# First pair's lam products on VectorE, and four W1 blocks of the next pair in places of product 7's operand

## The chip, the cores and the metric

The kernel runs on 1 core of a Trainium2 chip. The metric is the device time of one execution in microseconds (us). The engines are TensorE (PE; PEld is its weight load), VectorE (DVE), ScalarE (ACT), GpSimd (POOL) and SyncE (SP); each works through its own queue in order.

## The reference

Grouped-query attention (batch 8, 16 query heads, 4 key heads, 384 tokens, head size 64), whose output is x, followed by an MLP block:

```
x   = softmax(q k^T / 8) v                 # as (8, 384, 1024)
a1  = alpha1 * x + beta1
tok = w_tok @ a1                           # over the 384 tokens
u   = x + lam * tok
a2  = alpha2 * u + beta2
ch  = relu(a2 @ w_ch1) @ w_ch2             # 1024 -> 4096 -> 1024
out = u + lam * ch
```

Inputs and output are float32; the kernel multiplies in bf16.

## The kernel before

**Pairs.** The eight batches are taken as four pairs. Each pair goes through two big products: the first one (a2 with W1) and the second one (hidden with W2). Both are made of seven smaller products, numbered 1 to 7, by a Strassen-like scheme: operands are summed or subtracted first, the results afterwards. The attention and the token step of the next pair (function `side`) are woven into the second product of the current one, piece by piece, so that TensorE always has something to do.

**The order is written by hand.** `put(ps, phase, at, function, ...)` files a call under pair `ps`, phase 0 (first product) or 1 (second product) and step `at`. `steps(ps)` runs the pair's generator, and after each step runs what is filed under its number. In the first pair's second product (`second_product`, matmuls C L752) there are 21 turns of four steps: a turn is one product number and one third of the tokens (`turns`), with 16 matmuls of 128x512. Turns 9 to 20 are products 3, 6, 7 and 4, so product 4 has steps 72 to 83. Batch 3 (`C` side of the next pair) is filed 38 steps later than its table says: its step 22 is step 60 of the phase.

**The side's work.** Per piece p of 128 columns: scores (L260) and exponentials (ACT L269), attention output (L295), on DVE the reciprocal L300, x L303 and a1 L309, then the token matmuls `tok` (L324, L328), and on DVE L331 (u) and L334 (a2, in `obuf`). For some pieces of batch 3, `turn` transposes a2 on TensorE (L398) and ACT copies it out (L400). Scores, attention output, tokens and turns take turns on three PSUM banks (`three`), named sc in the trace. DVE also makes the sums of W2 blocks (`sum_w2`, L499), of the hidden (L603) and, near the end of the phase, of W1 blocks (`sum_w1`, L510 and L515) and of the turned a2 (`sums_a`, L448 to L450).

**Results.** ACT copies product sums to hT (L764) or back into a PSUM bank (L744), and DVE adds (L767). Finished parts are appended to `later`. `flush` takes them from there: `scaled` multiplies a 128x512 part by lam in place (L790) and `store` adds it to the output in memory with an accumulating DMA on POOL's queue (L442). In the first pair (`lead`) the product L790 is POOL's, in later pairs DVE's. Of the first pair's twelve parts, nine are flushed in its second product: the first three, of product 2, as soon as they can be, then those of products 6 and 7 from turn 17 on. The three of product 4 are flushed in the next pair's first product, one in each of its groups 1, 2 and 3.

**W1 blocks.** The next pair's first product (L831) needs 16 W1 blocks of 128 x 8 x 256 in the order `order1` = 0, 8, 1, 9, 2, 10, 3, 11, 4, 12, ..., two for each of its eight groups of 9.1 us. `load_w1` (L183) casts a block from memory into one of six slots of the ring `w1`, by a DMA on POOL's queue. Loads wait in `queue`, and `pump` issues the next one when a slot is freed. The W2 blocks of the second product use the same ring and three slots of `pad`.

**Product 7's operand.** The sums for the first pair's product 7 lie in `home(0)` to `home(3)`, four places of 128x2048 at the end of `arena`. The last read of them is in turn 17. The next pair's hidden is written over them in its groups 6 and 7.

Of the kernel before, what the change touches and what calls it, by code (L numbers as in the profile page):

```python
# [13 lines left out]
def kernel(  # L14
# [21 lines left out]
    nc = tc.nc  # L36
# [4 lines left out]
    MUL = mybir.AluOpType.mult  # L41
# [8 lines left out]
    P = 128  # L50
# [125 lines left out]

    w1src = moe_w_ch1.rearrange("(dt di) nf -> di dt nf", di=P)
    w2src = moe_w_ch2.rearrange("(nt ni) d -> ni nt d", ni=P)
    w1_slots, w1_free = {}, list(range(RING))

    def load_w1(c):
        w1_slots[c] = w1_free.pop(0)
        nc.gpsimd.dma_start(out=w1[:, w1_slots[c]], in_=w1src[:, :, c * CW * P:(c + 1) * CW * P])  # L183

    def bank(shape, tag, name, dtype=f32):
        if tag == "mm":
# [27 lines left out]
    def side(b):  # L214
# [192 lines left out]
        def put(k, *m):  # L407
            at.setdefault(k, []).append(m)
# [3 lines left out]
        for p in range(NP):  # L412
            put((4, 10, 14, 18, 24, 29, 33, 35)[p], av, p)
            put((8, 15, 17, 22, 27, 32, 36, 38 if b % 2 else 39)[p], tok_flip, p)
            if by_pe(p):
                put(((13, 20, 22, 28, 34, 37, 40, 42) if b == 3 else (0, 0, 0, 0, 0, 36, 39, 41))[p], turn, p)
        return at

    def loads(b):
# [84 lines left out]
        free(raw["12", c][0])  # L504

    def sum_w1(g, o):
        a, c = w1[:, w1_slots[g]], w1[:, w1_slots[g + NCH // 2]]
        H1, H2 = slice(0, NDT // 2), slice(NDT // 2, NDT)
        if o == 7:
            tt(out=c[:, H1], in0=c[:, H2], in1=c[:, H1], op=SUB)  # L510
            tb[g, 7], tb[g, 1], tb[g, 2], tb[g, 3] = c[:, H1], a[:, H1], a[:, H2], c[:, H2]
            return
        tb[g, o] = t = piece().rearrange("p (a c) -> p a c", a=NDT // 2)
        x, y = {5: (c[:, H1], a[:, H1]), 6: (c[:, H2], tb.get((g, 5))), 4: (a[:, H2], tb.get((g, 6)))}[o]
        tt(out=t, in0=x, in1=y, op=SUB)  # L515
# [58 lines left out]
    for name, cs, slots in (("12", (0, 1), w1_free), ("12", (2, 3), pad_free), ("22", (0,), pad_free), ("22", (1, 2, 3), w1_free),  # L574
                            ("again", (0,), w1_free), ("again", (1,), pad_free), ("again", (2, 3), w1_free)):
        queue += [(load_w2, name, c, slots) for c in cs]
    queue += [(load_w1, c) for c in order1[:4]]
    for i in range(1, NB):
        heads = [(load_w1, c) for c in order1[:4]] if i + 1 < NB else []
        queue += [(load_w1, c) for c in order1[4:]] + [(fetch, i, n) for n in range(SLOTS - 2)] + heads[:2]  # L580
        queue += [(fetch, i, n) for n in (SLOTS - 2, SLOTS - 1)] + heads[2:]

    IDENT = mybir.ActivationFunctionType.Identity
# [144 lines left out]
    def second_product(acc, later, flush, scaled):  # L728
        pad_free[:] = [RING + 1, RING, RING + 2]
        pump()  # L730
        s2, s1, s5, s3 = ([snaps[:, (NST * i + ms) * 512:(NST * i + ms + 1) * 512] for ms in range(NST)] for i in range(4))
        names = {1: "11", 2: "21", 3: "22", 5: "12", 6: "12", 7: "11", 4: "again"}
        xs_ = {}
        turns = ((1, 0), (1, 1), (2, 0), (2, 1), (1, 2), (5, 0), (2, 2), (5, 1), (5, 2),
                 *((o, ms) for o in (3, 6, 7, 4) for ms in range(NST)))

        def begin(o, ms):
            if o == 2:
                xs_[o, ms] = xs_[1, ms]
                return  # L740
            xs_[o, ms] = x = acc.tile([P, 512], f32, tag="acc", name="C", bufs=2)
            under = {3: s5, 6: s1, 7: s1, 4: s1}.get(o)
            if under:
                nc.scalar.copy(out=x, in_=under[ms])  # L744

        for k, (o, ms) in enumerate(turns):
            if (o, ms) not in xs_:
                begin(o, ms)
            x = xs_[o, ms]
            for t in range(NH):  # L750
                slot, rhs = raw[names[o], t // 4]
                nc.tensor.matmul(out=x, lhsT=lead_hid[:, t, FIRST2[o], ms * P:(ms + 1) * P],  # L752
                                 rhs=rhs[:, t % 4 * 512:(t % 4 + 1) * 512], start=(o in (1, 5) and t == 0), stop=(t == NH - 1),
                                 skip_group_check=True)
                if t % 4 == 3 and ms == NST - 1 and (o in (2, 3) or o == 4 and slot < RING):
                    free(slot)
                if t % 4 == 3 and t < NH - 1:
                    if t == 7 and turns[k + 1:] and turns[k + 1][0] in (3, 6, 7, 4):
                        begin(*turns[k + 1])
                    if t % 8 == 3 and later and (later[0][1] == 1 or k > 16 and later[0][1] != 4):  # L760
                        flush(1)
                    yield 1
            to = {1: s1, 2: s2, 5: s5, 3: s3, 6: s1, 7: s1, 4: s3}[o][ms]
            nc.scalar.copy(out=to, in_=x)  # L764
            if o in (6, 7):
                to, base = (s2[ms], s3[ms]) if o == 6 else (s5[ms], s5[ms])
                tt(out=to, in0=x, in1=base, op=ADD)  # L767
            if o in (2, 6, 7, 4):
                later.append((scaled, 1 if o == 2 else o, int(o in (7, 4)), ms, int(o in (6, 7)), to))
            yield 1  # L770

    def pair(i):
# [14 lines left out]

        def scaled(o, b, ms, dw, t):
            if o != 2 or not last:
                (nc.gpsimd if lead else nc.vector).tensor_tensor(out=t, in0=t, in1=lam_t[:, dw * 512:(dw + 1) * 512], op=MUL)  # L790
            store(b, ms, dw, t)

        def flush(n=9):
# [24 lines left out]
        for g in range(NH // 2):  # L818
            X, Y, snap = {}, {}, {}
            for k, (o, e) in enumerate(SEQ1):  # L820
                t = 2 * g + e
                lo, hi = bias1[:, t:t + 1], bias1[:, NH + t:NH + t + 1]
                if o == 1:
                    X[e] = pairs["X"].tile([P, 512], f32, tag="X", name="X", bufs=2)
                if o == 7:
                    Y[e] = pairs["Y"].tile([P, 512], f32, tag="Y", name="Y", bufs=2)
                if o == 2:
                    Z = pairs["Z"].tile([P, 512], f32, tag="Z", name="Z", bufs=4)
                ps = (X[e] if o in (1, 6, 5, 3) else Y[e] if o in (7, 4) else Z)[:, :S]
                for dt in range(NDT // 2):  # L830
                    nc.tensor.matmul(out=ps, lhsT=tb[g, o][:, dt, e * P:(e + 1) * P], rhs=opb(LEFT1[o])[:, dt],  # L831
                                     start=(o in (1, 2, 7) and dt == 0), stop=(dt == NDT // 2 - 1), skip_group_check=True)
                if o in (1, 6, 5):
                    q = ((2 if g % 2 else 8) + 2 * (1, 6, 5).index(o) + e) % 12 * S
                    snap[o, e] = snaps[:, q:q + S]
                    nc.scalar.activation(out=snap[o, e], in_=ps, func=IDENT, bias=hi if o == 5 else lo)  # L836
                if o == 5:
                    tt(out=hid[:, t, 1], in0=Y[e][:, :S], in1=snap[5, e], op=ADD)  # L838
                elif o == 2:
                    tt(out=hid[:, t, 0], in0=ps, in1=snap[1, e], op=ADD)  # L840
                elif o == 3:
                    nc.scalar.activation(out=hid[:, t, 4], in_=ps, func=RELU, bias=hi)  # L842
                elif o == 4:
                    tt(out=hid[:, t, 2], in0=ps, in1=snap[6, e], op=ADD)
                if k == 7 and 0 < g < 4:
                    flush(1)
                if (o, e) in ((2, 1), (3, 1)):
                    free(w1_slots.pop(g if o == 2 else g + NCH // 2))
                if k == 3 and g == 0:
                    tt(out=opb(6), in0=opb(4), in1=opb(5), op=SUB)  # L850
                if k == 2 and g == 0:
                    sum_w1(0, 4)
                if k in (2, 5, 8, 11) and g + 1 < NH // 2:
                    sum_w1(g + 1, {2: 5, 5: 7, 8: 6, 11: 4}[k])
                ts = slice(2 * g, 2 * g + 2)
                if k == 1 and g:
                    finish(slice(2 * g - 2, 2 * g))
                if (o, e) == (3, 1):
                    nc.scalar.activation(out=hid[:, ts, 1], in_=hid[:, ts, 1], func=RELU)
                if (o, e) == (4, 1):  # L860
                    nc.vector.tensor_scalar(out=hid[:, ts, 2], in0=hid[:, ts, 2], scalar1=0.0, scalar2=None,
                                            op0=mybir.AluOpType.max)
                    tt(out=hid[:, ts, 3], in0=hid[:, ts, 2], in1=hid[:, ts, 1], op=ADD)
                yield 0
# [82 lines left out]
    with tc.manual_schedule(engines=order):  # L947
# [150 lines left out]
        for c in range(4):  # L1098
# [8 lines left out]
            put(0, 1, (44, 45, 49, 50)[c], sums_first_hid, 3, c)  # L1107
            put(0, 1, (51, 54, 57, 58)[c], sum_w2, 7, c)
            put(0, 1, (61, 64, 68, 71)[c], last_w2, c)
        for u, o in ((77, 5), (79, 7), (81, 6)):  # L1110
            put(0, 1, u, sum_w1, 0, o)
        for ps in range(NB - 1):
# [101 lines left out]
```

## Time and profile before

| what | us |
|---|---|
| median of 3 runs | 732.27 |
| their range | 731.28 to 734.06 |
| the profiled execution | 731.92 |
| its span, first to last instruction | 729.9 |
| first pair's second product, first to last matmul (L752) | 129.9 to 234.4 |
| second pair's first product begins (L831) | 234.4 |

The span is what the profiler sees of the core; the execution's own time is 2.0 us longer. The granted TensorE clock is 1.00 throughout. In the tables, a row gives an engine, its source line and operation, what it writes and reads, and the mean time of one. Idle time is put down to what ended it.

### The profile page before, as it was taken

Reading aid. Unit: us, or ns where it says so; the run is one execution under the profiler, and the core shown is the slowest. Engines: PE = TensorE matmul, PEld = TensorE weight load, DVE = VectorE, ACT = ScalarE, POOL = GpSimd, SP = SyncE. Lnnn points to the kernel's source line nnn. Section 1 sums busy time; section 2 is a strip of 40 time slices with the busy share of each in tenths; the row PEclk is TensorE's granted clock in tenths of the full one; section 3 lists DMA queues with packets and bytes.
Section 4 is the critical chain, followed back from the end, with each engine's and each line's share of the span. In section 5 each row is a group of like instructions: output and inputs, shape, how many; then the busy total and the mean of one; then the engine's idle time right before and its main releaser. Section 6 shows DMA issues by size and latency. Waiting matters only on the chain.

```text
span 729.9 us, 14511 instructions
## 1 busy us (share of the span) xinstructions
PE 717.4 (98%) x5716; PEld 408.7 (56%) x5716; DVE 543.9 (75%) x1009; ACT 373.8 (51%) x566; POOL 199.2 (27%) x242
## 2 busy tenths in 40 slices
PE   8899999999999999999999999999999999999998
PEld 4665555555555666555555566655555566654444
DVE  7888876577888988649678888748868988763354
ACT  7877666544563666643433466663333366650000
POOL 8844233221046551201022344200002222000011
PEclk9999999999999999999999999999999999999999
DMA  9999999999999999969989999998989999937965
GB/s 164 180 239 231 190 195 227 226 242 235 366 312 232 179 182 196 234 221 207 272 193 220 160 162 194 212 227 201 270 233 183 210 126 146 165 123 264 302 174 104
DMA packets 197616, 153.26 MB, mean 210 GB/s; under 512 B 90540, under 2 KB 175892, under 8 KB 197292
## 3 DMA queue, kind: packets, MB, share of 16 engines
q0 software_dynamic: 109872, 64.47, 65.4%
q1 hardware_dynamic: 86988, 87.42, 42.8%
q8 instruction: 44, 0.72, 0.4%
q10 hardware_dynamic: 688, 0.46, 0.2%
q14 instruction: 24, 0.20, 0.1%
HBM read 155.23 MB, written 39.85 MB: 267 GB/s over the span
## 4 chain that ended last, share of the span: by engine, by line
PE 90%; DVE 4%; POOL 2%; DMA 1%; issue 1%; ACT 1%; DVEq 0%; ACTq 0%; POOLq 0%
PE C L897 30%; PE X L831 17%; PE C L752 10%; PE Y L831 9%; PE Z L831 4%; PE sc L260 4%; PE X L681 4%; PE sc L295 3%; PE sc L324 3%; PE Y L681 3%; DMA ops<-obuf 1%; DVE pad L565 1%; PE Z L681 1%; PE tok L324 1%; POOL obuf L334 0%
## 5 line engine op out<-in xcount | busy, mean ns | idle before, releaser
L897 PE MATMUL C<-w,arena 128*128 128x512 bf16 (+2 forms) x744 | 168.3, 372 | 0.0
L269 ACT ACTIVATE es<-sc 128x1024 bf16<-128x1024 f32 x108 | 104.1, 1024 | 116.0 <-PE sc L260 107.6
L897 PEld LDWEIGHTS <-arena 128*128 128x128 bf16 x1040 | 94.8, 98 | 100.5 <-issue 5.1
L442 POOL DMA_DIRECT2D out_dram<-hT x45 | 40.0, 888 | 294.7 <-DVE hT L790 135.9
L836 ACT ACTIVATE hT<-X,bias 128x384 f32<-128x384 f32 x144 | 83.6, 582 | 60.0 <-PE X L831 55.2
L831 PEld LDWEIGHTS <-w 128*128 128x128 bf16 x768 | 75.1, 98 | 50.0
L831 PEld LDWEIGHTS <-pad 128*128 128x128 bf16 x576 | 56.4, 98 | 37.2
L183 POOL DMA_DIRECT2D w<-in_moe_w_ch_dram x48 | 45.4, 1002 | 105.6 <-PE X L831 36.5
L831 PE MATMUL X<-ops,w 128*128 128x384 bf16 x384 | 70.3, 326 | 0.0
L831 PE MATMUL X<-ops,pad 128*128 128x384 bf16 x384 | 70.3, 326 | 0.0
L897 PE MATMUL C<-pad,arena 128*128 128x512 bf16 (+2 forms) x296 | 70.2, 373 | 0.0
L324 PEld LDWEIGHTS <-wtokT 128*128 128x128 bf16 x576 | 39.0, 98 | 16.4 <-issue 3.4
L752 PEld LDWEIGHTS <-arena 128*128 128x128 bf16 x336 | 29.8, 98 | 30.0 <-issue 2.5
L331 DVE TENSOR_TENSOR xr<-sc,xr 128x384 f32<-128x384 f32 x48 | 26.5, 553 | 25.6 <-PE sc L324 14.3
L752 PE MATMUL C<-w,arena 128*128 128x512 bf16 x168 | 41.2, 379 | 0.0
L838 DVE TENSOR_TENSOR arena<-Y,hT 128x384 bf16<-128x384 f32 x48 | 26.5, 556 | 17.7 <-ACT hT L836 16.0
L295 PEld LDWEIGHTS <-es 128*128 128x128 bf16 x864 | 32.8, 97 | 11.3
L831 PE MATMUL Y<-ops,w 128*128 128x384 bf16 x192 | 39.1, 326 | 0.0
L831 PE MATMUL Z<-ops,w 128*128 128x384 bf16 x192 | 39.0, 326 | 0.0
L269 ACT ACTIVATE hT<-sc 128x1024 bf16<-128x1024 f32 x36 | 35.8, 1031 | 4.3 <-PE sc L260 4.0
L260 PE MATMUL sc<-qT,kT 64*128 64x384 bf16 (+2 forms) x504 | 37.2, 271 | 0.5 <-ACT hT L269 0.2
L842 ACT ACTIVATE arena<-X,bias 128x384 bf16<-128x384 f32 x48 | 27.9, 582 | 17.7 <-PE X L831 16.1
(190 smaller groups left out, 1175.1 us busy)
## 6 DMA issues: line engine op xcount, KB each, us to landing
w<-w2s SPq DMA_DIRECT2D x67, 512.0 KB, 5.1
w<-in_moe_w_ch_dram POOLq DMA_DIRECT2D x65, 512.0 KB, 9.8
pad<-w2s SPq DMA_DIRECT2D x25, 512.0 KB, 6.9
out_dram<-hT POOLq DMA_DIRECT2D x45, 256.0 KB, 7.1
out_dram<-xr SPq DMA_DIRECT2D x48, 192.0 KB, 5.3
q_raw<-in_q_dram POOLq DMA_DIRECT2D x28, 192.0 KB, 9.5
w2s<-w SPq DMA_DIRECT2D x10, 512.0 KB, 7.6
arena<-in_moe_w_ch_dram POOLq DMA_DIRECT2D x8, 512.0 KB, 15.9
```

The source lines that it names most:

```text
L183: nc.gpsimd.dma_start(out=w1[:, w1_slots[c]], in_=w1src[:, :, c * CW * P:(c + 1) * CW * P])
L260: nc.tensor.matmul(out=sc[:, hh, k % 4:k % 4 + n], lhsT=kT_[r, 2 * p // G, BLK[hh][sk], :], rhs=qT_[r, p, st:st + n, :], start=True, stop= ...
L269: nc.scalar.activation(out=e, in_=sc, func=EXP, scale=scale_qk)
L295: nc.tensor.matmul(out=av[:, hh, sq, :], lhsT=ess[k // 4][:, m % 2, k % 4, :], rhs=vb[:, sk, hk, :], start=(sk == 0), stop=(sk == NST - 1))
L324: nc.tensor.matmul(out=ps[:, tt, :], lhsT=wtokT[:, st, tt * P:(tt + 1) * P], rhs=a1s[p][:, st, :], start=(st == 0), stop=(st == NST - 1 an ...
L442: nc.gpsimd.dma_start(out=by_tok(out[b])[:, ms, dw * 512:(dw + 1) * 512], in_=o, accum_op=ADD)
L681: nc.tensor.matmul(out=ps[:, :n], lhsT=tb[G, o][:, dt, e * P:(e + 1) * P], rhs=opb(FIRST1[o], n)[:, dt], start=(o in (1, 2, 7) and dt == 0 ...
L752: nc.tensor.matmul(out=x, lhsT=lead_hid[:, t, FIRST2[o], ms * P:(ms + 1) * P], rhs=rhs[:, t % 4 * 512:(t % 4 + 1) * 512], start=(o in (1, ...
L831: nc.tensor.matmul(out=ps, lhsT=tb[g, o][:, dt, e * P:(e + 1) * P], rhs=opb(LEFT1[o])[:, dt], start=(o in (1, 2, 7) and dt == 0), stop=(dt ...
L836: nc.scalar.activation(out=snap[o, e], in_=ps, func=IDENT, bias=hi if o == 5 else lo)
L842: nc.scalar.activation(out=hid[:, t, 4], in_=ps, func=RELU, bias=hi)
L897: nc.tensor.matmul(out=x, lhsT=hid[:, t, LEFT2[o], ms * P:(ms + 1) * P], rhs=rhs[:, t % 4 * 512 + c0:t % 4 * 512 + c1], start=((not last o ...
```

## The change

Five edits. `scaled` always multiplies on VectorE, in the first pair too. The parts of products 6 and 7 are flushed from turn 16 on instead of 17. Blocks 9, 2, 10 and 3 of W1 are loaded into `home(0)` to `home(3)` at steps 72 to 75 of the first pair's second product; the ring then takes only blocks 0, 8 and 1 before, and 11 and the rest after them. `w1_at` says where a block lies, and `free_w1` frees a ring slot only if the block had one. The turn of piece 2 of batch 3 is filed one step later.

```diff
-    w1_slots, w1_free = {}, list(range(RING))
-
-    def load_w1(c):
-        w1_slots[c] = w1_free.pop(0)
-        nc.gpsimd.dma_start(out=w1[:, w1_slots[c]], in_=w1src[:, :, c * CW * P:(c + 1) * CW * P])
+    w1_slots, w1_at, w1_free = {}, {}, list(range(RING))
+
+    def load_w1(c, at=None):
+        if at is None:
+            w1_slots[c] = w1_free.pop(0)
+            at = ring[:, w1_slots[c]]
+        w1_at[c] = at.rearrange("p (a c) -> p a c", a=NDT)
+        nc.gpsimd.dma_start(out=w1_at[c], in_=w1src[:, :, c * CW * P:(c + 1) * CW * P])
+
+    def free_w1(c):
+        if c in w1_slots:
+            free(w1_slots.pop(c))
...
-                put(((13, 20, 22, 28, 34, 37, 40, 42) if b == 3 else (0, 0, 0, 0, 0, 36, 39, 41))[p], turn, p)
+                put(((13, 20, 23, 28, 34, 37, 40, 42) if b == 3 else (0, 0, 0, 0, 0, 36, 39, 41))[p], turn, p)
...
-        a, c = w1[:, w1_slots[g]], w1[:, w1_slots[g + NCH // 2]]
+        a, c = w1_at[g], w1_at[g + NCH // 2]
...
-    queue += [(load_w1, c) for c in order1[:4]]
+    queue += [(load_w1, c) for c in order1[:3]]
...
-        queue += [(load_w1, c) for c in order1[4:]] + [(fetch, i, n) for n in range(SLOTS - 2)] + heads[:2]
+        queue += [(load_w1, c) for c in order1[4 if i > 1 else 7:]] + [(fetch, i, n) for n in range(SLOTS - 2)] + heads[:2]
...
-                    if t % 8 == 3 and later and (later[0][1] == 1 or k > 16 and later[0][1] != 4):
+                    if t % 8 == 3 and later and (later[0][1] == 1 or k > 15 and later[0][1] != 4):
                         flush(1)
...
-                (nc.gpsimd if lead else nc.vector).tensor_tensor(out=t, in0=t, in1=lam_t[:, dw * 512:(dw + 1) * 512], op=MUL)
+                nc.vector.tensor_tensor(out=t, in0=t, in1=lam_t[:, dw * 512:(dw + 1) * 512], op=MUL)
...
-                    free(w1_slots.pop(g if o == 2 else g + NCH // 2))
+                    free_w1(g if o == 2 else g + NCH // 2)
...
+        for c in range(4):
+            put(0, 1, 72 + c, load_w1, order1[3 + c], home(c))
```

On the engines' queues this moves twelve products from POOL to DVE, four loads on POOL ahead of others, and one turn on TensorE (with its copy L400 on ACT) behind a token step; SP's queue keeps its order.

## The prediction

> **What bounds the kernel now.** I read the page first, then a table of busy time by stage over the whole span, then TensorE's waits there, then the timeline around them. The page says who is the bound:
>
> ```profile
> span 729.9 us, 14511 instructions
> ...
> PE 717.4 (98%) x5716; PEld 408.7 (56%) x5716; DVE 543.9 (75%) x1009; ACT 373.8 (51%) x566; POOL 199.2 (27%) x242
> ```
>
> TensorE is idle for 729.9 - 717.4 = 12.5 us in all, so no change that leaves its work alone can bring more than that. The table by stage tells where the idle time lies. About 4.4 us are in the first 30 us, 3.7 us in the last 10 us, 2.8 us between 50 and 120 us, and 1.8 us in the end of the first pair's second product, 198 to 234.4 us. From 234.4 us to 720 us every stretch is full. The change edits only 140 to 300 us. Rows of that stretch (columns: width, then busy us and instruction count of PE, PEld, DVE, ACT, POOL; granted clock, DMA share, GB/s):
>
> ```profile
> 198.00:210.00 12.00, 11.41 (x113) 6.20 (x112) 10.54 (x17) 6.02 (x10) 1.79 (x2) 1.00 1.14 330
> 210.00:222.00 12.00, 11.76 (x123) 6.77 (x118) 9.99 (x13) 8.81 (x13) 8.96 (x8) 1.00 1.23 284
> 222.00:234.40 12.40, 11.45 (x94) 6.34 (x93) 12.09 (x23) 3.55 (x8) 6.24 (x7) 1.00 1.07 249
> 234.40:246.40 12.00, 12.00 (x75) 7.22 (x74) 8.82 (x14) 7.96 (x14) 6.85 (x10) 1.00 1.36 177
> ```
>
> The clock is 1.00, PE is short of the width by 0.6, 0.2 and 0.95 us, and VectorE is at 83 to 97%. TensorE's waits from 195 to 236 us are these three, and no more:
>
> ```profile
> PE sc L324 <- DVE a L309: 0.9, 1, 0.9
> PE sc L324 <- ACT es L269: 0.6, 1, 0.6
> PE sc L398 <- ACT es L269: 0.2, 1, 0.2
> ```
>
> The timeline shows what stands around the first of them (start, duration, engine, line; idle before in brackets):
>
> ```profile
> 220.24 1.55 POOL L790 TENSOR_TENSOR hT<-hT,vecs 128x512 f32<-128x512 f32 x1
> ...
> 220.87 2.02 DVE L499 TENSOR_TENSOR w<-w,pad 128x2048 bf16<-128x2048 bf16 x1
> ...
> 222.71 1.57 POOL L790 TENSOR_TENSOR hT<-hT,vecs 128x512 f32<-128x512 f32 x1
> ...
> 223.62 1.08 DVE L309 TENSOR_TENSOR a<-xr,vecs 128x384 bf16<-128x384 f32 x1
> ...
> 224.76 0.34 PE L324 MATMUL sc<-a,wtokT 128*128 128x128 bf16 x3 [0.95 <-DVE a L309]
> ```
>
> L499 takes 1.22 us elsewhere and L309 0.56 us. Here they overlap a lam product (L790) on GpSimd and end 0.4 to 1.1 us after it. The same holds for L334 at 212.75 us (1.77 instead of 0.56), L309 at 216.14 us (0.93) and L309 at 225.44 us (1.74). Between 209 and 228 us the stretch adds up to 1.2 + 0.4 + 0.8 + 0.5 + 1.2 = 4.1 us of VectorE time. L303 at 223.03 us, with a PSUM input, kept its 0.56 us beside an L790, and L499 at 217.00 us, beside a store's issue alone, its 1.21 us.
>
> **The lam products.** All 12 leave GpSimd. Their price is in the rows of L790, which VectorE already runs for the later pairs:
>
> ```profile
> L790 DVE TENSOR_TENSOR hT<-hT,vecs x30: 679/684/693, 328.6 to 716.4; 128x512 f32<-128x512 f32 x30
> L790 POOL TENSOR_TENSOR hT<-hT,vecs x12: 1263/1559/2112, 142.8 to 263.6; 128x512 f32<-128x512 f32 x12
> ```
>
> So GpSimd gives up 18.6 us, and VectorE takes on 12 x 0.684 = 8.2 us (0.61 us from start to start, as L767, of the same size, shows at 209.56 and 210.17 us). In the order of the changed kernel three stand between 142 and 166 us, six between 209 and 227 us, three in the next pair's first product. The six cost VectorE 6 x 0.61 = 3.7 us and take away 4.1 us of slowed instructions: even.
>
> I replay VectorE's queue with start-to-start times of undisturbed rows (L300 0.23, L303 0.59, L309 0.47, L331 0.59, L334 0.47, L499 1.14, L767 and L790 0.61). L309 at 208.86 us is the last that stays, since L499 at 204.10 us waits 1.10 us for a DMA and all behind it follows. Then come L767 at 209.33, L790, L499, L331 at 211.69, L334, L790, L767 at 213.96 (it waits for ScalarE's copy L764), L300, L303, L309 at 215.39, L790, L499, L790, L331 at 218.22, L334, L767 at 219.5, L499, L300, L303 and the critical L309 at 222.07, done at 222.63 instead of 224.70 us. TensorE is ready for it when the four matmuls from 222.78 us have issued: 222.78 + 0.86 = 223.64 us; less the 0.75 us of the next part it is 222.89 us. It therefore gets the whole 224.76 - 223.64 = 1.12 us, with 0.2 us to spare. (The wait list says 0.95, because a matmul's recorded end lies after its issue slot.) The last sums before the next product (L449 at 233.92, needed by PE at 235.68) move by about 1.7 us and PE by 1.9, so that cover of 1.4 us stays. The first three products stand at 143.7, 149.7 and 164.0 us. They delay L499 by nothing, L331 by 0.2 and L300 by 0.9 us. The token matmul behind the last one runs at 168.43 us and L309 would end at 167.4: price zero, cover 1 us. The three in the next pair stand at 245 to 270 us, where the 2.9 us of the next but one part are free again and the sums are wanted a group (9.1 us) later: zero.
>
> The Trainium skill, page "SBUF — State Buffer", section "SBUF: two separate sides", says that VectorE and GpSimd share one port pair under an exclusive lock, and that a VectorE op with two SBUF inputs is held for the whole of a GpSimd op that reads SBUF. By that rule the slow rows go with the products on GpSimd, the sum is the one below, and the last rival falls; the trace agrees as far as the undisturbed L303 and L499 show it.
>
> **The moved turn.** The transpose of token piece 2 of batch 3 (step 22 to 23) goes behind the token matmuls L324 of piece 3 and four product matmuls. Now it takes the first of three PSUM banks, and the token matmuls take the second, which an exponential (L269) frees at 204.85 us. The order written in that step is C at 203.01 us (0.86), turn (0.17), tokens at 204.89: TensorE could have gone on at 203.87, so 1.02 - 0.17 = 0.85 us are lost. Swapped, the tokens take the bank freed at about 203.92 us, wait 0.1 us, and the turn comes at 205.5 us, when its bank is long free. Gain 0.75 us. On ScalarE the turn's eviction L400 goes behind copy L744, which waits for VectorE's L767 (end 205.93): its bank is free at 207.1 us instead of 206.1, and the next scores begin at 208.9. The third wait (0.2 in the list, 0.4 in issue slots at 221.20 us) hangs on L269 behind L764 on ScalarE, follows TensorE, and stays.
>
> **The W1 blocks.** The number of loads (L183, 0.9 us of GpSimd each) is the same. Blocks 9, 2, 10 and 3 went out at 232.10, 234.32, 235.2 and 242.0 us, when ring slots came free. Now they are queued on GpSimd at steps 72 to 75, behind the eighth store L442, which waits for its product on VectorE (223.2 us), so at some 223 to 228 us. VectorE's wait of 2.92 us at 238.07 us (L515 for block 9) goes, but TensorE has no idle time there: gain zero on the path, 2.9 us of VectorE's headroom. Against it, 2 MB more are in flight before 234 us. The stretch moves 249 to 330 GB/s, 376 were reached from 180 to 190 us, and nothing that TensorE waits for there is a transfer; bound 0 to 1 us. I take 0. Reading the blocks from arena instead of the ring costs nothing: a weight load takes 98 ns from w, pad and arena alike, and L752 takes 379 ns with its operand in either place. SP's order is unchanged.
>
> **Sum.** 0.75 + 1.12 = 1.87 us. The profiled execution took 731.92 us (span 729.9 and 2.0 around it): 730.05. It lies 0.35 us below the median of the runs, 732.27, so on that scale 730.4 us.
>
> **Rivals.** *Only one wait goes*: the replay has only 0.2 us to spare, and a bank may come free later than I think. 732.27 - 0.75 = 731.5, or - 1.12 = 731.15. *Nothing is gained*: the waits re-form behind ScalarE (L400 now after L744); for it speaks that ScalarE is 50 to 73% busy there, against it that its copies had idle time before them. 732.3. *VectorE becomes the bound* (the other side): if the slowed rows are not GpSimd's doing but, say, the transfers', the 4.1 us stay and 3.7 us come on top. Of the four products ahead of the critical L309 (2.4 us), 2.0 us fill VectorE's idle time, so it ends at 225.1; the next L309, two products later, ends at 228.8 instead of 227.18, and TensorE's second token step moves from 227.33 to 228.8 us: 1.5 us later, 732.27 + 1.5 = 733.8. It decides once the critical L309 ends after 224.7. Against it stand the undisturbed L303 and L499 named above.
>
> On the page "Perfetto Trace Analysis", section "Optimizing Scalar/DVE Operations", the Trainium skill says that work of a saturated VectorE may be offloaded to GpSimd, which speaks against this change, but adds that the two share a port. By the first half the last rival is right, by the second my sum; the rows above bear the second out.
>
> *The change does not do what it says*: the loads start no sooner because GpSimd's queue holds them behind stores. Then 238 us looks as before, at no cost to the time; this lies within the first case.
>
> **How the numbers follow.** Both waits gone 0.62 (730.4; the third wait too, at most 0.4 less), one of them 0.17 (731.3), nothing 0.09 (732.3), VectorE the bound 0.09 (733.8), something unforeseen 0.03. The three runs scatter from 1.0 below to 1.8 above their median. The range reaches from 730.4 - 0.4 - 1.0 = 729.0 to 731.4 + 1.8 = 733.2. About what a measurement can tell from no change is 0.5%, 3.66 us (728.6 and 735.9). TensorE's idle time in the edited stretch is 1.8 us in all, so faster than that comes from scatter alone, 0.04; slower needs the VectorE case with scatter or the unforeseen, 0.04.
>
> **What would show it.** Right: the row 222 to 234 without PE's wait on L309, L309 and L334 back at 0.56 us, L499 at 1.22, the token matmuls starting right behind their C matmuls, L515's wait on a W1 block gone, the next product's first L831 at about 232.5 us. Wrong: a new wait of PE on L309 or on the turn's L400 between 200 and 234 us, or any idle time of PE between 234 and 300 us.

## The result and the profile after

The changed kernel takes 739.12 us (median of five runs, 736.62 to 740.59), against 732.29 us (731.28 to 734.06) for five runs of the kernel before: a ratio of 1.008, with a 95% interval of 1.0053 to 1.0107. It is slower by somewhat more than the 0.5% that can be told from no change. The profiled execution is the one of 739.12 us. Its span is 737.3 us, 7.4 us longer than before.

From here on line numbers are those of the changed kernel. Lines from L190 on stand 7 higher than before, and L183, the load of a W1 block, is L186:

| before | changed | what |
|---|---|---|
| L831, L836, L850 | L838, L843, L857 | first product: matmul; ScalarE's copy of a sum; VectorE's subtraction for operand 6 |
| L790, L442, L183 | L797, L449, L186 | lam product; accumulating store; load of a W1 block |
| L309, L499, L515 | L316, L506, L522 | a1; a sum of W2 blocks; a sum of W1 blocks |

**What came as forecast.** The page of the changed kernel shows twelve more instructions on DVE and twelve fewer on POOL:

```profile
span 737.3 us, 14442 instructions
...
PE 717.0 (97%) x5657; PEld 410.1 (56%) x5716; DVE 541.0 (73%) x1021; ACT 373.7 (51%) x566; POOL 181.7 (25%) x230
```

DVE's busy time fell, from 543.9 to 541.0 us, although it has twelve products more. The timeline of the changed kernel shows why. Instructions that had been slow beside POOL's products have their undisturbed duration (start, duration, engine, line):

```profile
221.35 1.22 DVE L506 TENSOR_TENSOR w<-w,pad 128x2048 bf16<-128x2048 bf16 x1
...
223.30 0.56 DVE L316 TENSOR_TENSOR a<-xr,vecs 128x384 bf16<-128x384 f32 x1
```

Before, these rows had 2.02 and 1.08 us. All 42 lam products now take 0.68 us. The row 222 to 234.4 us of the table by stage is full on PE (12.29 of 12.40 us, before 11.45); the idle time lies in the next row (columns as in the prediction):

```profile
222.00:234.40 12.40, 12.29 (x99) 7.00 (x99) 11.94 (x26) 4.43 (x9) 7.00 (x8) 1.00 1.17 249
234.40:246.40 12.00, 6.79 (x32) 3.57 (x31) 2.85 (x6) 3.50 (x7) 1.79 (x3) 0.79 1.40 201
```

**What did not.** TensorE's waits from 200 to 255 us in the changed kernel. The two priced ones (on a1, and 0.6 us on the exponential) are gone, and a long one stands ahead of all others:

```profile
PE X L838 <- ACT hT L843: 5.2, 1, 5.2
PE sc L267 <- DVE xr L310: 0.7, 1, 0.7
```

The timeline of the changed kernel tells the story behind it, on three engines:

```profile
225.32 2.11 POOL L186 DMA_DIRECT2D arena<-in_moe_w_ch_dram  x2
227.13 1.25 POOL L449 DMA_DIRECT2D out_dram<-hT  x1
...
238.40 0.69 DVE L522 TENSOR_TENSOR pad<-arena,w 128x1024 bf16<-128x1024 bf16 x1 [3.89 <-DMA arena<-in_moe_w_ch_dram]
239.01 0.95 DVE L857 TENSOR_TENSOR ops<-ops 128x1536 bf16<-128x1536 bf16 x1
...
242.38 1.05 ACT L843 ACTIVATE hT<-X,bias 128x384 f32<-128x384 f32 x2 [6.56 <-DMA out_dram<-hT]
...
243.01 2.72 PE L838 MATMUL X<-ops,pad 128*128 128x384 bf16 x8 [5.21 <-ACT hT L843]
```

Two early loads, blocks 9 and 2, are issued on POOL's queue at 225.32 us, ahead of the ninth accumulating store (227.13 us). ScalarE's copy L843 keeps a sum of the new product in hT. For product 6 of group 0 it writes places 10 and 11 of hT, and there lies the part of product 7 that this store still reads. So the copy waits until the store has landed, and TensorE waits for the copy, because the next matmuls go into the bank that it reads. The chain of waits of the changed kernel has the store's flight in one piece:

```profile
227.13 15.17 DMA out_dram<-hT
```

In the kernel before, the same store went out at 227.05 us with no W1 load between it and the store before. The accumulating stores between 205 and 262 us landed after 7.5 to 13.5 us there (median 9.8; now 7.1 to 15.2, median 13.1), and nobody waited. The kernel before, at the same place:

```profile
227.05 0.87 POOL L442 DMA_DIRECT2D out_dram<-hT  x1 [0.30 <-POOL hT L790]
...
232.10 0.92 POOL L183 DMA_DIRECT2D w<-in_moe_w_ch_dram  x1 [4.17 <-PE sc L398]
...
238.07 0.69 DVE L515 TENSOR_TENSOR pad<-w 128x1024 bf16<-128x1024 bf16 x1 [2.92 <-DMA w<-in_moe_w_ch_dram]
238.68 0.95 DVE L850 TENSOR_TENSOR ops<-ops 128x1536 bf16<-128x1536 bf16 x1
...
240.23 1.46 PE L831 MATMUL X<-ops,w 128*128 128x384 bf16 x8
```

The wait is not all. Here is TensorE in stretches of 2 us in the changed kernel (width, busy us and matmuls, granted clock, DMA share, GB/s):

```profile
240.00:242.00 2.00, 0.00 (x0) 0.84 1.34 195
242.00:244.00 2.00, 0.98 (x4) 0.50 1.46 198
...
248.00:250.00 2.00, 2.00 (x13) 0.95 1.45 197
```

The clock is 0.50 from 241.4 to 248.2 us (0.84 and 0.95 are the two ends of it), 5 us of which lie behind the restart. The 24 matmuls from 243.01 to 249.45 us take 6.44 us; before, the same ones took from 238.28 to 242.18 us, 3.90. **The account:** the product starts 0.64 us earlier (233.74 for 234.38 us), TensorE stands for 5.4 us (in issue slots: 237.64 to 243.01), the half clock costs 2.5 us, and 0.1 to 0.2 us lie elsewhere; together 7.4 us, the difference of the spans. The clock averaged over the execution is 0.994 or 0.995 in all five runs of the changed kernel; 6.8 us at half clock in 737 us give 0.995, so all five had a drop of about this size, though only the profiled one shows where.

### The profile page after: what moved, and what is told of

Same layout as the page of the kernel before. It is cut to its first block, busy times and chain, and to the rows that moved or that the text cites. A ratio compares the mean times of both kernels' runs of the same rounds, so it can differ in the third digit from the quotient of the medians.

```text
span 737.3 us, 14442 instructions
## 1 busy us (share of the span) xinstructions
PE 717.0 (97%) x5657; PEld 410.1 (56%) x5716; DVE 541.0 (73%) x1021; ACT 373.7 (51%) x566; POOL 181.7 (25%) x230
## 4 chain that ended last, share of the span: by engine, by line
PE 83%; DVE 6%; DMA 5%; POOL 2%; issue 2%; ACT 1%; DVEq 0%; POOLq 0%; ACTq 0%; SPq 0%
PE C L904 28%; PE X L838 17%; PE Y L838 8%; PE C L759 6%; PE Z L838 4%; PE sc L267 4%; PE X L688 4%; PE sc L302 3%; PE Y L688 3%; PE sc L331 3%; DMA out_dram<-hT 2%; DMA w<-in_moe_w_ch_dram 2%; DMA w2s<-arena 1%; PE E L620 1%; PE tok L331 1%
## 5 line engine op out<-in xcount | busy, mean ns | idle before, releaser
L904 PE MATMUL C<-w,arena 128*128 128x512 bf16 (+2 forms) x711 | 163.7, 372 | 1.6 <-issue 0.3
L449 POOL DMA_DIRECT2D out_dram<-hT x45 | 39.8, 885 | 337.4 <-DVE hT L797 171.9
L843 ACT ACTIVATE hT<-X,bias 128x384 f32<-128x384 f32 x144 | 83.6, 582 | 66.5 <-PE X L838 55.2
L838 PEld LDWEIGHTS <-w 128*128 128x128 bf16 x704 | 69.4, 99 | 46.9 <-issue 1.7
L838 PEld LDWEIGHTS <-pad 128*128 128x128 bf16 x576 | 56.7, 98 | 43.2 <-issue 6.4
L838 PE MATMUL X<-ops,pad 128*128 128x384 bf16 x384 | 71.5, 330 | 5.2 <-ACT hT L843 5.2
L186 POOL DMA_DIRECT2D w<-in_moe_w_ch_dram x44 | 42.2, 1014 | 100.2 <-DVE rinv L307 43.8
L838 PE MATMUL X<-ops,w 128*128 128x384 bf16 x352 | 65.1, 328 | 0.0
L759 PEld LDWEIGHTS <-arena 128*128 128x128 bf16 x336 | 29.8, 98 | 30.6 <-issue 3.4
L845 DVE TENSOR_TENSOR arena<-Y,hT 128x384 bf16<-128x384 f32 x48 | 26.7, 557 | 25.4 <-ACT hT L843 23.6
L759 PE MATMUL C<-w,arena 128*128 128x512 bf16 x159 | 39.9, 379 | 0.5
L838 PE MATMUL Z<-ops,w 128*128 128x384 bf16 x176 | 36.5, 331 | 0.0
L838 PE MATMUL Y<-ops,w 128*128 128x384 bf16 x176 | 35.8, 326 | 0.0
```

What stands on the lines that cost most here:

```text
L186: nc.gpsimd.dma_start(out=w1_at[c], in_=w1src[:, :, c * CW * P:(c + 1) * CW * P])
L449: nc.gpsimd.dma_start(out=by_tok(out[b])[:, ms, dw * 512:(dw + 1) * 512], in_=o, accum_op=ADD)
L904: nc.tensor.matmul(out=x, lhsT=hid[:, t, LEFT2[o], ms * P:(ms + 1) * P], rhs=rhs[:, t % 4 * 512 + c0:t % 4 * 512 + c1], start=((not last o ...
```

## The experiments

**Theory:** the early loads, by their place on POOL's queue ahead of the ninth store, make it land late, and ScalarE's copy over its source stops TensorE; the idle time then halves the clock. **Rivals:** the 2 MB more in flight slow everything, wherever they are queued; or VectorE's order is at fault, since the subtraction L857 stands behind the sum L522 that waits for block 9, so that TensorE waits there as soon as the product starts earlier; or the lam products or the turn do harm of their own.

Three of the fourteen profiled runs (e4, e9 and e12) have a wait of 5.5 to 7.0 us for the transposed q at 33 to 35 us, far outside the edited stretch. The kernel before scatters as widely (731.30 to 740.09 us on one chip); that the same wait does it there is not shown, since its one profile has none. So the table gives the stages of the profiled runs beside the ratios: the first pair's second product (first L759 to first L838; in the kernel before from its first L752 at 128.07 us, not 129.9, to 234.38), the next pair's first product (to the first matmul of its second), TensorE's waits in that one, and the ratio to the kernel before on the same chip with its 95% interval. The stages are of one profile each.

| run | 2nd product | next 1st product | PE waits in it | ratio |
|---|---|---|---|---|
| before | 106.3 | 72.8 | none | 1 |
| changed | 106.1 | 80.7 | 5.2 on L843 | 1.008 (1.0053 to 1.0107) |
| e1_other_places | 105.8 | 73.9 | 1.0 on L857 | 0.9978 (0.9951 to 1.0004) |
| e2_loads_behind | 104.4 | 74.9 | 1.9 on L857 | 1.0004 (0.9978 to 1.003) |
| e3_no_early_loads | 104.4 | 75.4 | 2.0 on L857 | 1.0009 (0.998 to 1.0037) |
| e4_early_loads_only | 105.7 | 84.5 | 8.3 on L843 | 1.0199 (1.0163 to 1.0236) |
| e5_turn_only | 107.9 | 72.8 | none | one run |
| e6_lam_only | 105.2 | 79.3 | 2.7 on L857, 1.4 on L851 | one run |
| e7_one_ahead | 104.4 | 75.9 | 2.9 on L843 | 1.0033 (1.0005 to 1.0062) |
| e8_four_ahead | 108.2 | 86.6 | 11.0 on L843 | 1.0196 (1.0158 to 1.0233) |
| e9_places_and_sum_first | 105.9 | 72.8 | none | 1.0012 (0.9979 to 1.0045) |
| e10_no_loads_sum_first | 104.4 | 73.9 | 0.5 on L845, 0.3 on L851 | 1.0014 (0.9984 to 1.0044) |
| e11_before_sum_first | 106.3 | 73.3 | none | 0.9998 (0.9979 to 1.0017) |
| e12_filled_wait | 104.8 | 78.7 | 0.6 on the copy, 5.4 filled | 1.0042 (1.0012 to 1.0072) |

### Which part does it

**e1_other_places**: the changed kernel, but in the second pair the copies of even and odd groups swap places in hT, so that group 0 doesn't touch the part of the ninth store.

```
-  q = ((2 if g % 2 else 8) + 2 * (1, 6, 5).index(o) + e) % 12 * S
+  q = ((2 if (g + (i == 1)) % 2 else 8) + 2 * (1, 6, 5).index(o) + e) % 12 * S
```

> The changed kernel, but in the second pair alone ScalarE's copies of the first product (L843) begin with the other half of their twelve places in hT, those whose stores went out 10 us earlier. The queues are untouched. Theory (late store: the ninth accumulating store of the first pair lies behind two W1 loads on GpSimd's queue, lands at 242 us, and the copy that overwrites its place waits for it): the store lands as late as before, but nothing waits; PE's 5.2 us wait and the half clock behind it go, 731 us (730 to 732.5). Rival 1 (VectorE, with 12 more products, is what is late, and the store only the last in name): 739 us. Rival 2 (2 MB more in flight slow every transfer, whatever the order): 731 to 733 us, as the theory, since here too only the copy waits; e2 and e4 part those two.

731.84 us, against 733.67 for the kernel before on that chip. The stores landed as late as ever (10.8 to 15.9 us, median 14.4), but no one waited for them, and in the profiled run the clock stayed at 1.00. Only the place was altered, so the wait is on the place, and the late landing and the 2 MB in flight by themselves cost nothing that can be told from the scatter. TensorE's wait in the product that is left is the second rival's:

```profile
PE X L838 <- DVE ops L857: 1.0, 1, 1.0
```

**e2_loads_behind**: the changed kernel with the four loads two steps later, behind the ninth store.

```
-  put(0, 1, 72 + c, load_w1, order1[3 + c], home(c))
+  put(0, 1, 74 + c, load_w1, order1[3 + c], home(c))
```

> The changed kernel with the four early loads filed two steps later (74 to 77), so that all four stand behind the ninth store on GpSimd's queue. Theory: the store lands some 8 to 10 us after its issue at 227 us, as in the kernel before, at 235 to 237 us; the copy needs the place at about 237 us; no wait or under 1 us; 731 us (730 to 732.5). Rival 1 (VectorE late): 739 us. Rival 2 (bytes in flight, not the order): the store still takes 15 us, wait of about 5 us, 738 to 739 us.

734.24 against 733.67 us. The ninth store, issued at 225.23 us, landed after 10.0 us, ScalarE waited 0.7 us for it, and TensorE not at all, as the theory has it. The waits of e2:

```profile
PE X L838 <- DVE ops L857: 1.9, 1, 1.9
...
ACT hT L843 <- DMA out_dram<-hT: 0.7, 1, 0.7
```

But the 731 us expected did not come. Block 9 was used at 238.62 us all the same, and TensorE waited 1.9 us for L857 behind it.

**e3_no_early_loads**: the changed kernel without its loads: the lam products and the turn alone.

```
-  queue += [(load_w1, c) for c in order1[:3]]
+  queue += [(load_w1, c) for c in order1[:4]]
...
-  for c in range(4):
-      put(0, 1, 72 + c, load_w1, order1[3 + c], home(c))
```

> The changed kernel without the four early loads: lam products on VectorE, flushing from turn 16, the moved turn; blocks 9, 2, 10 and 3 go through the ring as in the kernel before. Theory: no stall at the start of the second pair's first product, 731 us (730 to 732). Rival 1 (VectorE late): 738 to 739 us. Rival 2 (bytes in flight): as the theory.

733.75 against 733.67 us. The next product begins at 232.20 us, 2.2 earlier than before; the prediction had 232.5. But the time is that of the kernel before and not the 731 us expected, for the gain goes to the second rival's wait. The timeline of this run:

```profile
238.78 0.69 DVE L522 TENSOR_TENSOR pad<-w 128x1024 bf16<-128x1024 bf16 x1 [5.81 <-DMA w<-in_moe_w_ch_dram]
239.39 0.95 DVE L857 TENSOR_TENSOR ops<-ops 128x1536 bf16<-128x1536 bf16 x1
240.40 1.48 PE L838 MATMUL X<-ops,w 128*128 128x384 bf16 x8 [2.04 <-DVE ops L857]
```

Block 9 does not come earlier because the product does. It was there at 238.78 us, before at 238.07, and L857, which needs no W1 block, goes behind the sum that does. Before, the subtraction ended at 239.63 us and TensorE came for it at 240.23: a cover of 0.6 us, and a start 2.2 us earlier uses it up.

**e4_early_loads_only**: the kernel before with the early loads alone (lam products on POOL, flush from turn 17, turn at step 22).

```
   (the loads, w1_at and free_w1 of the change; not its other edits)
+  for c in range(4):
+      put(0, 1, 72 + c, load_w1, order1[3 + c], home(c))
```

> The kernel before with the early loads alone: lam products stay on GpSimd, flushing from turn 17, the turn at its old step. Two loads then stand ahead of the seventh store, four ahead of the eighth and ninth. Theory: the ninth store goes out and lands still later (246 us or more), the wait at the start of the second pair's first product is longer than 5.2 us, 741 to 744 us. Rival 1 (VectorE late): VectorE has nothing more to do, 732 to 733 us. Rival 2 (bytes in flight): about the same wait as in the changed kernel, 739 to 740 us.

748.37 against 733.67 us. The early loads alone make the harm, more of it than in the whole change and than expected (741 to 744 us): ScalarE waits for stores three times (10.4 us), TensorE twice (3.0 and 5.3 us). 5.5 us of this profiled run's excess are the wait at 33 us; the next pair's first product has 11.7 us.

**e5_turn_only** and **e6_lam_only**: the kernel before with the turn at step 23, and with the lam products on VectorE, each alone.

```
e5:  -  (13, 20, 22, 28, ...)          +  (13, 20, 23, 28, ...)
e6:  -  (nc.gpsimd if lead else nc.vector).tensor_tensor(out=t, in0=t, ...
     +  nc.vector.tensor_tensor(out=t, in0=t, ...
```

> The kernel before with the moved turn alone. By the prediction's step the first pair's second product gets 0.75 us shorter (106.3 to 105.5 us from its first matmul to the next product's first), unless the following wait (L324 for L309) takes part of it; what is won is given back if the subtraction L857 still stands behind block 9.

> The kernel before with the lam products on VectorE alone (flushing still from turn 17). By the prediction's step PE's wait on L309 goes, 1.1 us, the stage takes 105.2 us; L309, L334 and L506 keep 0.56, 0.56 and 1.22 us. With the products flushed one turn later, some stand between the last L309 and L338, so part of it may come back.

733.9 us (e5) and 736.82 us (e6), one run each, against a median of 733.14 us. In e5 the wait of 0.6 us on the exponential is gone. But a sum of W2 blocks (L506) waited 2.5 us for a store of a W2 block, and TensorE waited for a1 (1.7 us, before 0.9) and x (0.7), so 107.9 us says nothing for or against the 0.75 us. In e6 the wait on a1 is gone and the stage is 105.2, 1.1 us shorter, which is the price that the prediction gave it. Then TensorE stands for L857 again. The windows of e6 (columns as above) show that this wait, of 2.7 us only, was followed by the half clock:

```profile
242.00:244.00 2.00, 2.00 (x11) 0.73 1.46 193
244.00:246.00 2.00, 2.00 (x8) 0.50 1.20 130
246.00:248.00 2.00, 2.00 (x13) 0.92 1.25 165
```

So the lam products alone, flushed from turn 17, can do harm by the second rival's way: block 9, issued at 231.76 us behind the ninth store, lands at 240.04. Together with the earlier flush and the turn, in e3, they do none that is clear of the scatter.

### How much per load

**e7_one_ahead** and **e8_four_ahead**: the changed kernel with one of the loads ahead of the ninth store, and with all four.

```
e7:  +  put(0, 1, 73 + c, load_w1, order1[3 + c], home(c))
e8:  +  put(0, 1, (72, 72, 73, 73)[c], load_w1, order1[3 + c], home(c))
```

> The changed kernel with the early loads one step later (73 to 76): one W1 load ahead of the ninth store, not two. Late-store theory: the copy's wait lies between the 0.7 us with none ahead and the 6.6 us with two, at about 3.5 us, PE's wait on it at 2 us with little or no half clock; 734 to 736 us. If bytes in flight and not the order delay the store, the wait is that of the changed kernel, 739 us.

> The changed kernel with the early loads at steps 72, 72, 73, 73: all four ahead of the ninth store. Late-store theory: some 3 us more wait for each load ahead, 12 us on the copy, 11 us on PE, then the half clock: 744 to 747 us. If bytes in flight and not the order matter: 739 us.

734.41 and 747.69 us, against 732.66. TensorE's and ScalarE's waits in e7:

```profile
PE X L838 <- ACT hT L843: 2.9, 1, 2.9
...
ACT hT L843 <- DMA out_dram<-hT: 4.0, 1, 4.0
```

With 0, 1, 2 and 4 loads ahead (e2, e7, the change, e8) the ninth store takes 10.0, 13.4, 15.2 and 16.8 us from issue to landing, and ScalarE waits 0.7, 4.0, 6.6 and 11.9 us. The order decides, load by load; the four loads are the same in all four kernels.

The landings (issue plus time to landing) show the price of one. In the changed kernel POOL's transfers land in the order of issue and at an even pace: block 9 at 238.31 us, block 2 at 240.97, the ninth store at 242.30, blocks 10 and 3 at 244.93 and 247.56. So a load takes about 2.65 us of this queue's time, and the store 1.3 us. In e8 the four loads ahead land at 243.28, 245.98, 248.62 and 251.25 us and the store at 252.59, at the same pace. Its issue was late there (235.76 us, since the fourth load waited 1.8 us on POOL for a turn, L405), but the even pace shows no delay from that.

### The second wait, and the half clock

**e9_places_and_sum_first**, **e10_no_loads_sum_first**, **e11_before_sum_first**: e1, e3 and the kernel before, with the subtraction moved one matmul group ahead, in front of the sum of block 9.

```
-                if k == 3 and g == 0:
-                    tt(out=opb(6), in0=opb(4), in1=opb(5), op=SUB)
                 if k == 2 and g == 0:
+                    tt(out=opb(6), in0=opb(4), in1=opb(5), op=SUB)
                     sum_w1(0, 4)
```

> e1 (the other half of hT for the second pair's copies) and, on VectorE, the subtraction for product 3's operand (L857) put ahead of the sums of W1 blocks (L522) instead of behind the one that waits for block 9. Theory (block 9 lands at 238.5 us whatever is done, and the subtraction stands behind it in VectorE's queue): PE's wait of 1.0 us on L857 goes too, the second pair's first product has no wait; 730.5 us on the scale of 732.3 for the kernel before, ratio 0.9975. Rival (PE also waits for something else at that place, such as the sum itself): as e1, ratio 0.998 to 0.999 with a wait of 1 us under another name.

> e3 (no early loads) with the same subtraction put first. Theory: in e3 the product began 2.2 us earlier than in the kernel before, and PE gave 2.0 us back waiting for L857 behind block 9; now nothing is given back, ratio 0.997 to 0.9975 (some 2 us below the kernel before). Rival (the early start is lost at another wait, for the stores or for block 9's own sum): ratio 0.999 to 1.001.

> The kernel before with the subtraction for product 3's operand put ahead of the W1 sums on VectorE, as in e9 and e10, and nothing else. There its end (239.63 us) lies 0.6 us ahead of the matmul that needs it (240.23), so nothing waits: no change, ratio 1.000; its effect in e9 and e10 comes only with the earlier start.

733.13 (e9; against 732.66), 734.29 (e10; 732.66) and 731.9 us (e11; 733.14): none is told from the kernel before, so the ratio of 0.9975 expected of e9 and e10 did not come. In e9 no wait is left in the product, 72.8 us; but its profiled run has 7.0 us of the wait at 33 us, and its runs reach from 729.26 to 740.05 us, so the 0.5 us that its two stages are shorter are lost in the scatter. In e10 the wait on L857 is gone, and another has its place, by sums of the hidden (L845, L851) that stand behind L522 as well. The waits of e10:

```profile
PE Y L838 <- DVE arena L845: 0.5, 1, 0.5
PE Y L838 <- DVE arena L851: 0.3, 1, 0.3
```

So e10's expectation held for L857 and missed for the stage (73.9 us). In e11 nothing was to be had, since TensorE did not wait there before.

**e12_filled_wait**: the changed kernel, with 32 matmuls of no use (their sums are read by no one) in the place where TensorE waits.

```
+  if i == 1 and g == 0 and k == 6:
+      fill = pairs["Z"].tile([P, 512], f32, tag="Z", name="fill", bufs=4)
+      for n in range(32):
+          nc.tensor.matmul(out=fill[:, :S], lhsT=wtokT[:, 0, :P], rhs=wtokT[:, 1, :], start=True, stop=True)
```

> The changed kernel with 32 matmuls of 128x384 on data that lie ready (their product is not used) put into TensorE's queue just ahead of the matmul that waits for the late store; 32 x 0.163 = 5.2 us, the length of the wait. If the half clock after the wait is the price of TensorE standing idle: the clock stays at 1.00, the 5.3 us that ran at half clock (243 to 248 us) take 2.65, stage from L838's first to L904's first matmul 78 us instead of 80.7, 736.5 us. If the clock falls for another reason: still 0.5 after the wait, 739 us.

736.08 against 733.14 us. ScalarE still waits for the store (7.2 us), and TensorE's waiting time is filled. The timeline of e12:

```profile
244.00 5.36 PE L840 MATMUL fill<-wtokT 128*128 128x384 bf16 x32
249.92 1.46 PE L842 MATMUL X<-ops,pad 128*128 128x384 bf16 x8 [0.56 <-ACT hT L847]
```

The clock is 1.00 in every window from 236 to 256 us, and the product takes 78.7 us instead of 80.7: 2.0 us by doing more work, near the 2.5 us of the account. The two ratios' intervals overlap, so this rests on the stage and the clock: averaged over the execution it is 0.999 or 1.000 in nine of the ten runs of e12 (the tenth, the profiled one, has the wait at 33 us), against 0.994 or 0.995 in all five of the changed kernel.

## Why the prediction was wrong, point by point

- **"Nothing that TensorE waits for there is a transfer; bound 0 to 1 us. I take 0."** This term failed, with 5.4 us of idle time and 2.5 of half clock. It asked what bytes the loads add, and bounded that by GB/s; e1 shows no cost of the bytes and late landings themselves. It did not ask what stands behind the loads on POOL's queue: a store, and behind the store, through the place in hT, a copy, a bank and TensorE. Its text names the loads as queued "behind the eighth store", but not the ninth behind them. The Trainium skill, page "DMA: Bandwidth & Descriptors", section "Two DMAs through the same engine are not ordered", says that within one queue of a DMA engine descriptors (the pieces of a transfer) start in order; the four store times of e2, e7, the change and e8 agree.
- **"VectorE's wait of 2.92 us … goes, but TensorE has no idle time there: gain zero on the path."** The wait did not go; it is 3.9 us. Block 9 was issued at 225.3 us instead of 232.1, and used at 238.40 instead of 238.07: 13 us of flight for 6. From 205 to 250 us W1 loads take 15.0 us (median) to land, before 9.3. An early issue on a queue that is behind does not mean an early landing: in e2 block 9 is issued 4.1 us earlier than in e3 (225.80 for 229.91 us) and lands 0.2 us earlier (238.52 for 238.69). The rival "the change does not do what it says" was thus half right, but the loads were held up in the queue's transfers and not by GpSimd's issuing, and at a price.
- **Covers of the next product.** The sum let the product start 1.9 us earlier and looked at one cover (the last sums, 1.4 us). L857's cover of 0.6 us was left out. e3 shows what follows: even without the loads, a start 2.2 us earlier ends in a wait of 2.0 us. So without the loads, too, the time would have stayed at that of the kernel before (ratio 1.0009) instead of the 730.4 us forecast.
- **The lam products and the turn** were sized rightly. In e2, e3, e7 and e10 the stage is 104.4 us, 1.9 below 106.3; e6 alone has 1.1 of the 1.12, and the turn's 0.75 is shown only as the rest, since e5 could not tell. The replay held too: in e3, where VectorE's queue runs 0.36 us earlier, the critical a1 begins at 221.76 us, against 222.07 - 0.36 = 221.71. In the changed kernel's own profile the stage gained only 0.2 us, since two sums L506 waited 3.2 us there for a store of a W2 block (before 1.1). The change, e1, e2 and e7 are the same program up to step 72 and have 3.2, 2.9, and in e2 and e7 0.6 to 1.6 us, so this differs from run to run of the same edits; whether the change adds to it, the two profiles with 1.1 and 1.0 us (before, e11) cannot say.
- **"VectorE becomes the bound"**, the rival on the slower side, had the wrong mechanism: L316 and L506 have their undisturbed times, in the changed kernel and in e6, with the lam products alone. This agrees with the rule that the prediction took from the Trainium skill's page "SBUF — State Buffer", section "SBUF: two separate sides": with POOL's products gone, the slow rows of VectorE are gone. One row was misread: L499 at 217.00 us did not stand beside a store's issue alone. A lam product began at 217.59 us, inside it, and it was the product that was the longer one (1.74 us; the next two took 1.55 and 1.57).
- **The range.** Its upper end, 733.2 us, is added up from a 731.4 that stands nowhere else in the prediction, and lies below the 733.8 of a rival with a chance of 0.09. Neither decided: 739.12 us is far above both.
- **The sign named for "wrong"**, idle time of PE between 234 and 300 us, is what came.

What stays open: no version here beats both kernels by more than the scatter. The ratio of e1 (0.9978) reaches up to 1.0004, and its stages are not shorter than those of the kernel before; in e9 no wait is left, and the 0.5 us of its stages are hidden by the wait at 33 us. Where that wait comes from was not tried.

## What to carry to other kernels

Before a transfer is put ahead on a queue, list what is queued behind it, and for each store among these, who next writes over what it reads: that writer waits until the store has landed. When an edit lets a stage start earlier, everything in it that hangs on a transfer stays where it was, and so does all that stands behind it on an in-order engine; work that needs no transfer belongs ahead of such a wait. Price a new wait of TensorE of about 3 us (2.7 us was enough in e6) with the chance of a stretch of half clock on top.

## What was not expected of the hardware

The stretches at clock 0.50 come in whole multiples of 3.41 us, read from the ends of the windows: 242.9 to 246.3 in e6 (one), 241.4 to 248.2 in the changed kernel (two), 245.2 to 255.4 in e4 (three), 244.7 to 258.3 in e8 (four). A wait of 2.7 us was enough in e6, while 2.0 us in e3 and 2.9 us in e7 had no drop in the profiled runs. (Other runs of e7 have mean clocks of 0.997 and 0.998; one stretch would give 0.998.) In e6 TensorE was idle in only 2.2 of the 3.41 us before the drop (239.5 to 242.9 us). The Trainium skill, page "TensorE: Matmul & The Clock Gate", section "Part 1: The HAM clock gate", says that the clock is halved or restored by windows of about 3.4 us that run free of the program; the lengths agree, and with free windows a 2.7 us wait can fall where a 2.9 us one does not. The same page's advice, under "Why this matters for your kernels", to keep gaps below some 3 us, did not protect e6.
